# Layer norm of tokens 512 to 2047 from column tiles of x, and a written order for all five engines, in the opening of an attention and MLP kernel

## The chip, the core and the metric

The kernel runs on one core of a Trainium2 chip. Five engines work side by side, each through its own queue in order: PE (TensorE, matrix products), DVE (VectorE), ACT (ScalarE), POOL (GpSimd) and SP (SyncE, which here only issues transfers). The metric is the device time of one execution in microseconds (us); lower is better. Times of the trace count from the start of its span.

## The reference, cut to what matters

The input x has 2048 tokens of 512 features. It is normalised without weights, goes through attention of 32 heads with 16 features each and through an MLP with 1792 hidden features, and the two meet in a gate:

```python
xn = _layernorm(x, axis=-1)          # (x - mean) / sqrt(var + eps)
s = _A_ref(xn, A_wqkv, A_wo)         # softmax(q k^T / 4) v, then @ wo
g = _silu(_B_ref(xn, B_w1, B_b1, B_w2, B_b2))   # relu(xn @ w1 + b1)^2 @ w2 + b2
return x + s * g
```

Everything is float32. The kernel keeps that precision on PE by splitting each operand into a high part (rounded to PE's format) and a low part (the rest), and adds three products: high by high, high by low, low by high.

## The kernel before

**Layout.** The 2048 tokens form four chunks c of 512, and 16 tiles t of 128. For the products, the normalised x has to stand with its features on the partitions: `xTs[c]` holds, for a chunk, [128 partitions, high and low, 4 blocks of features (KO = 4), 512 tokens]. From it come q and k, by tiles ("qk", m, c) of 128 output rows (m = 0 to 3 is q, 4 to 7 is k, eight heads each), and v, by tiles ("v", c, tt) of 128 tokens. A tile is 12 matmuls of 512 columns (4 blocks by three products; L1207 for q and k, L1273 for v), and 24 of 256 columns for m = 0 and 4 of chunk 0.

**Opening, up to the first rounds.** SP loads 16 tiles of x (L1361, 256 KB each), and between them the weights `wm` (k and q of the first eight heads), `wv` (v) and later `wr` (the others). Each x tile has its tokens on the partitions and passes through this chain: statistics on DVE (`ln_stats`, L1369, L1371), square root on ACT (L1373), reciprocal and shift on DVE (L1378, L1379), normalisation on ACT (L1387; on DVE, L1383, for the first two tiles), four transposes on PE into a bank of PSUM (`ln_high`, L1394), the high part by ACT out of PSUM (L1396) and the low part by DVE (`ln_low`, L1402), which subtracts the high part from the bank. The weights are split by ACT and POOL (`split_w`, L1136, L1137, L116, L117). Between the transposes, `pump(n)` puts a few matmuls of the product tiles on PE, by a table of numbers for each tile. A done product tile is copied out of PSUM by ACT, split by POOL (`split`, L116 and L117: a copy to the high part, then a subtraction) or by ACT and DVE (`split_psum`, L122, L123), and stored to DRAM by SP (L1162, L1285).

**Order.** In this part the order of PE, ACT, DVE and POOL is as the code is written (`manual_schedule`); the queue of SP is ordered by a scheduler. SP's DMAs and, in the change, ACT's share eight semaphores in turn, so that a DMA waits until the one that had its semaphore before it has landed. By L1553 the twelve loads of k for the first four heads (`load_k`, L181, 128 KB each, 16 partitions) and those of q (`load_q_pair`, L170) are asked for; with them come the biases b1 and b2 (L1542, L1545).

**What follows.** From L1572 on come the rounds (`side_rounds`, L1303): PE is split into two row halves, on which the other product tiles go side by side with the first score tiles, whose maxima DVE takes (`max_mm`, L401, L408). The rounds need k of the first four heads in `kas` (tile ka) and q in `qms` (tile qm). Behind them the loop over 512 steps does scores, exp, the products with v, and the MLP between them. Rounds and loop are the same before and after the change.

The lines at which the opening hands a tile on:

```python
when_done(lambda: qk_done(m, c, ps, quick, 0))   # L1215: copy out, split, store
if i >= 4:
    pump({4: 6, 7: 14, 8: 12}.get(i, 8 if i < 7 else 7 if i < 11 else 6))
```

Of the kernel before, what the change touches and what calls it, by code (L numbers as in the profile page):

```python
# [9 lines left out]
F32 = mybir.dt.float32  # L10
# [63 lines left out]
def kernel(  # L74
    ctx: ExitStack,
    tc: tile.TileContext,
    x: bass.AP,
    wqkv: bass.AP,
# [18 lines left out]
    sp_d = dram.tile([S, D], F32, name="sp_d")  # L97
    xn_d = dram.tile([2, P, KO, S], F32, name="xn_d")
# [33 lines left out]
    with ExitStack() as ph:  # L132
# [42 lines left out]
        def load_k(qd, n):  # L175

            p, j, i = n // 6, n // 3 % 2, n % 3
            if n % 6 == 0:
                kas[qd, p] = ring("ka")
            h = 4 * qd + 2 * p + j  # L180
            nc.sync.dma_start(  # L181
                kas[qd, p][64 * j + DH * i : 64 * j + DH * (i + 1), :].bitcast(F32),
                k_d[h // 8][i % 2, (h % 8) * DH : (h % 8 + 1) * DH, :],
            )
# [13 lines left out]

        def load_q(u, name):
            tiles = []  # L200
            for p in range(2):
                load_q_pair(u, name, p, tiles)
            return tiles
# [928 lines left out]
        def split_w(dst, kos, cols, raw, pool=False):  # L1132
            if pool:
                split((dst[:, 0, kos, cols], dst[:, 1, kos, cols]), raw)
                return
            nc.scalar.activation(dst[:, 0, kos, cols], raw, AF.Copy)  # L1136
            nc.gpsimd.tensor_tensor(  # L1137
                dst[:, 1, kos, cols], raw, dst[:, 0, kos, cols].bitcast(F32), op=ALU.subtract
            )

        def load_w(name, width, at, kos=(KO,)):
            raw = st.tile([P, KO, width], F32, name=name)
            k0 = 0
            for n in kos:
                nc.sync.dma_start(
                    raw[:, k0 : k0 + n],
                    wqkv[:, at + k0 * width : at + (k0 + n) * width].rearrange(
                        "p (k n) -> p k n", n=width
                    ),
                )  # L1150
                k0 += n
            return raw
# [28 lines left out]
        held = []  # L1181
        hold = [True]

        def when_done(fn):
            if hold[0]:
                held.append(fn)
            else:
                fn()

        def let_go():  # L1190
            while held:
                held.pop(0)()

# [8 lines left out]
        def qk_tile(m, c):  # L1202
            ps = qkv_bank()

            for n0, n1 in ((0, 256), (256, 512)) if c == 0 and m % 4 == 0 else ((0, 512),):
                for out_, lh, rh, first_, last_ in qk_terms(m, c, ps):
                    nc.tensor.matmul(  # L1207
                        out_[:, n0:n1], lh(slice(0, P)), rh(slice(0, P))[:, n0:n1],
                        start=first_, stop=last_,
                    )  # L1210
                    if not last_ or n1 < 512:
                        yield
            quick = m % 4 == 0 and not hold[0]

            when_done(lambda: qk_done(m, c, ps, quick, 0))  # L1215
            yield

        def qk_done(m, c, ps, quick, wait):
            hl = hlp.tile([P, 2, 512], F32R, name="hl")
            if quick:  # L1220
                split_psum(hl[:, 0], hl[:, 1], ps)
            else:
                raw = hlp.tile([P, 512], F32, name="raw", bufs=2)
                nc.scalar.activation(raw, ps, AF.Copy)
                split((hl[:, 0], hl[:, 1]), raw)
            later(wait, lambda: qk_store(m, c, hl))
# [726 lines left out]
```

## Time and profile before

| | us |
|---|---|
| time, median of 3 runs (1571.22 to 1571.72) | 1571.31 |
| the profiled execution, its own time | 1571.16 |
| its span, from the first to the last instruction | 1569.3 |
| opening: up to the first round on PE (L1303) | 0 to 62.36 |
| rounds, about | 62 to 160 |
| loop and end | 160 to 1569.3 |

A row of the timeline gives start and duration in us, engine, line, operation, out<-in with shapes, and the count of merged instructions; in brackets how long the engine stood idle before, and what released it. In the table by stage each engine has its busy time and its count of instructions in the stretch, then come the granted clock of PE (1.00 is full), the share of time that the DMA engines were busy, and GB/s. In a row of the groups, busy time and mean duration in ns stand behind the bar. In a row of the waits stand the sum in us, how often, and the longest.

### The profile page before, as it was taken

To read this page: it belongs to the slowest core of one execution; us is meant where nothing else is said; L and a number is where in the kernel's file an instruction comes from. 1 tells how busy PE (TensorE), PEld (TensorE's weight loads), DVE (VectorE), ACT (ScalarE), POOL (GpSimd) and SP (SyncE) were. 2 spreads that over 40 slices of the span, in tenths; PEclk is the share of its full clock that TensorE was granted. 3 is DMA by queue.
4 is the path that set the end of the run, shared out by engine and by line. 5 is a ranking of instruction groups with operands and counts; after the bars stand their busy time and mean duration, and the time that the engine had idled before them with its cause. 6 is when DMAs were issued, how large, how long until landed. Compare 5 with 4: busy or idle time off the path is not lost.

```text
span 1569.3 us, 34206 instructions
## 1 busy us (share of the span) xinstructions
PE 1557.0 (99%) x12364; PEld 872.9 (56%) x12364; DVE 1342.3 (86%) x2307; ACT 1279.3 (82%) x2507; POOL 805.9 (51%) x824
## 2 busy tenths in 40 slices
PE   8999999999999999999999999999999999999998
PEld 7899755555555555555555555555555555555553
DVE  7377899999989998999899999998999999887765
ACT  7222788888889888888898888888888888888886
POOL 6346787348645543354465434545654345654621
PEclk9999999999999999999999999999999999999999
DMA  8967666224544531345244322533552143347665
GB/s 296 255 237 233 198 200 183 51 58 129 173 111 137 148 88 38 77 142 129 73 137 139 71 56 72 157 103 81 145 150 57 37 107 90 75 119 220 205 203 179
DMA packets 152216, 210.11 MB, mean 134 GB/s; under 512 B 58192, under 2 KB 71248, under 8 KB 150480
## 3 DMA queue, kind: packets, MB, share of 16 engines
q1 hardware_dynamic: 151904, 207.67, 46.5%
q8 instruction: 98, 1.61, 0.4%
q14 instruction: 70, 0.57, 0.1%
q10 hardware_dynamic: 144, 0.26, 0.0%
HBM read 141.56 MB, written 63.68 MB: 131 GB/s over the span
## 4 chain that ended last, share of the span: by engine, by line
PE 98%; DVE 1%; DMA 1%; issue 0%; ACT 0%; SPq 0%; DVEq 0%
PE se L487 17%; PE se L1434 12%; PE po L487 9%; PE pd_t L275 8%; PE pm_t L275 8%; PE pm_t L401 7%; PE pm_t L1434 7%; PE se L401 5%; PE pm_t L487 5%; PE pm_t L1303 4%; PE po L1434 4%; PE pd_t L401 2%; PE pm_t L243 2%; PE po L401 1%; PE pd_t L1303 1%; PE se L1273 1%
## 5 line engine op out<-in xcount | busy, mean ns | idle before, releaser
L408 DVE TENSOR_REDUCE mx<-pm_t 128x1 f32<-128x512 f32 x898 | 590.2, 682 | 50.3 <-PE pm_t L401 36.7
L1446 ACT ACTIVATE pt<-se 128x512 f32<-128x512 f32 x983 | 570.5, 623 | 30.4 <-PE pm_t L275 10.2
L408 DVE TENSOR_REDUCE mx<-se 128x1 f32<-128x512 f32 x716 | 478.3, 684 | 90.5 <-PE se L401 62.5
L1434 PE MATMUL se<-qe,ka 64*128 64x512 f32 x1086 | 434.4, 414 | 0.0
L401 PE MATMUL pm_t<-ka,qm 64*128 64x512 f32 x898 | 347.8, 398 | 0.0
L1446 ACT ACTIVATE pt<-pm_t 128x512 f32<-128x512 f32 x546 | 326.9, 622 | 8.9 <-PE pm_t L275 3.9
L1434 PEld LDWEIGHTS se<-qe,ka 64*128 64x128 f32 x1086 | 195.6, 184 | 201.6 <-ACT pt L1446 129.6
L487 PE MATMUL se<-pt,v 128*32 128x512 f32 x2224 | 282.1, 602 | 0.0
L401 PE MATMUL se<-ka,qm 64*128 64x512 f32 x716 | 281.8, 412 | 0.0
L1683 POOL TENSOR_TENSOR sum<-sum,sum 128x512 f32<-128x512 f32 x99 | 127.8, 1291 | 186.3 <-ACT sum L1682 185.9
L1683 POOL TENSOR_TENSOR ot<-ot,sum 128x512 f32<-128x512 f32 x99 | 127.7, 1290 | 180.2 <-ACT sum L1682 180.0
L1434 PE MATMUL pm_t<-qe,ka 64*128 64x512 f32 x575 | 219.0, 407 | 0.0
L275 PE MATMUL pm_t<-w2t,hT 64*128 64x512 f32 x780 | 206.6, 398 | 0.0
L1446 ACT ACTIVATE pt<-po 128x512 f32<-128x512 f32 x299 | 186.7, 625 | 7.8 <-PE pm_t L275 3.8
L401 PEld LDWEIGHTS pm_t<-ka,qm 64*128 64x128 f32 x898 | 164.0, 184 | 35.6 <-DVE mx L408 4.0
L275 PE MATMUL pm_t<-xc,w1s 64*128 64x512 f32 x672 | 177.3, 396 | 0.0
L275 PE MATMUL pd_t<-xc,w1s 64*128 64x512 f32 (+1 forms) x672 | 170.9, 388 | 0.0
L408 DVE TENSOR_REDUCE mx<-pd_t 128x1 f32<-128x512 f32 x233 | 158.7, 681 | 1.5 <-PE pd_t L401 1.5
L408 DVE TENSOR_REDUCE mx<-po 128x1 f32<-128x512 f32 x201 | 137.4, 683 | 22.2 <-PE po L401 18.7
L275 PE MATMUL pd_t<-w2t,hT 64*128 64x512 f32 x564 | 149.3, 397 | 0.0
L401 PEld LDWEIGHTS se<-ka,qm 64*128 64x128 f32 x716 | 131.4, 184 | 21.0 <-DVE mx L408 7.9
L275 PEld LDWEIGHTS pm_t<-w2t,hT 64*128 64x128 f32 x780 | 139.5, 184 | 4.4
(225 smaller groups left out, 2956.9 us busy)
## 6 DMA issues: line engine op xcount, KB each, us to landing
w1s<-w_d SPq DMA_DIRECT2D x84, 256.0 KB
w2t<-w_d SPq DMA_DIRECT2D x42, 512.0 KB
qm<-q_d SPq DMA_DIRECT2D x384, 32.0 KB
ka<-k_d SPq DMA_DIRECT2D x96, 128.0 KB
qe<-q_d SPq DMA_DIRECT2D x384, 32.0 KB
q_d<-hl SPq DMA_DIRECT2D x16, 512.0 KB
g<-g_d SPq DMA_DIRECT2D x32, 256.0 KB
k_d<-hl SPq DMA_DIRECT2D x15, 512.0 KB
```

What stands on the lines that cost most here:

```text
L243: mm = nc.tensor.matmul(out_() if callable(out_) else out_, lh(r), rh(r), start=first_ and lane == 0, stop=last_ and lane == 1, skip_group ...
L275: mm = nc.tensor.matmul(out_() if callable(out_) else out_, lh(r), rh(r), start=first_ and lane == 0, stop=last_ and lane == 1, skip_group ...
L401: nc.tensor.matmul(ps, qms[u][p][64 * j : 64 * j + 64, qb * P : (qb + 1) * P], kas[qd, p][64 * j : 64 * j + 64, kc * 512 : (kc + 1) * 512] ...
L408: return nc.vector.tensor_reduce(mxs[u][:, c, kc : kc + 1], ps, axis=AX.X, op=ALU.max)
L487: nc.tensor.matmul(po[32 * j : 32 * j + 32, :], vs[qd][:, (4 * kb + j) * VW : (4 * kb + j) * VW + 32], pts[j], start=first, stop=last, ski ...
L1273: nc.tensor.matmul(out_, lh(slice(0, P)), rh(slice(0, P)), start=first_, stop=last_)
L1303: mm = nc.tensor.matmul(out_, lh(r), rh(r), start=first_ and lane == first, stop=last_ and lane != first, skip_group_check=True,)
L1434: nc.tensor.matmul(se, kas[qd, j // 2][b : b + 64, kb * P : (kb + 1) * P], qes[u][j // 2][b : b + 64, :], start=True, stop=True,)
L1446: return nc.scalar.activation(pts[j], se, AF.Exp, scale=0.25)
L1683: nc.gpsimd.tensor_tensor(pos["sum"], pos["sum"], part, op=ALU.add)
```

## The change

Tokens 0 to 511 (tiles 0 to 3) keep the old way. Tokens 512 to 2047 come in six groups g of 256, each loaded twice: as rows (`load_rows`, tile xg, two tokens on a partition) for the statistics alone, and as columns (`load_columns`, tile xc, features on the partitions), out of a second copy of x that the host lays out that way. Mean and standard deviation are taken from the rows on DVE and ACT, written to DRAM (`row_out`, st_d) and read back spread over all partitions (`row_in`, sb, 256 KB), both from ACT's queue. DVE then subtracts and multiplies the columns in place (`column_norm`), ACT makes the high part and DVE the low part, both out of SBUF. No transposes are needed for these tokens.

The opening is now one list in which the calls of all engines stand in one order, SP's too. wv is split by ACT and POOL in place of POOL alone. All q and k tiles are split by POOL but ("qk", 4, 3), which ACT and DVE split out of PSUM. k of chunks 0 to 2 is loaded from DRAM in two steps (`load_k` with columns); that of chunk 3 goes straight from SBUF to SBUF (`move_k`), and half of the 24 transfers of the last step are issued by ACT. The copy of `xTs[0]` into ring ka and the biases are asked for behind them (`keep_first`, `load_bias`).

The new functions, and two stretches of the list:

```diff
+        def load_rows(g):
+            rows[g] = xp.tile([P, 2, D], F32, name="xg", bufs=3)
+            nc.sync.dma_start(
+                rows[g], xf[512 + g * 256 : 768 + g * 256, :].rearrange("(p j) d -> p j d", j=2)
+            )
+        def load_columns(g):
+            columns[g] = xp.tile([P, KO, 256], F32, name="xc", bufs=3)
+            nc.sync.dma_start(columns[g], xc[g])
+        def row_stats(g, j):
...
+            nc.vector.bn_stats(stats, rows[g][:, j])
+            nc.vector.bn_aggr(moments[g][:, :, j], stats)
+        def row_root(g):
+            m = moments[g][:, 1]
+            nc.scalar.activation(m, m, AF.Sqrt, bias=eps_t)
+        def row_scale(g):
+            m = moments[g][:, 1]
+            nc.vector.reciprocal(m, m)
+        def row_out(g):
+            nc.scalar.dma_start(st_d[g], moments[g])
+        def row_in(g):
+            spread[g] = xp.tile([P, P, 2, 2], F32, name="sb", bufs=3)
+            nc.scalar.dma_start(
+                spread[g].rearrange("p a s j -> p (a s j)"),
+                st_d[g].rearrange("a s j -> (a s j)")[None, :].to_broadcast([P, 512]),
+            )
+        def column_norm(g):
+            v = columns[g].rearrange("p k (a j) -> p k a j", j=2)
+            for i, op in enumerate((ALU.subtract, ALU.mult)):
+                nc.vector.tensor_tensor(
+                    v, v, spread[g][:, None, :, i, :].to_broadcast([P, KO, P, 2]), op=op
+                )
+        def column_high(g):
+            c, h = divmod(g + 2, 2)
+            nc.scalar.activation(
+                xTs[c][:, 0, :, h * 256 : (h + 1) * 256], columns[g], AF.Copy
+            )
+        def column_low(g, eng):
...
+            eng.tensor_tensor(
+                xTs[c][:, 1, :, sl], columns[g], xTs[c][:, 0, :, sl].bitcast(F32),
+                op=ALU.subtract,
+            )
+        def low_w(dst, kos, cols, raw):
             nc.gpsimd.tensor_tensor(
+                dst[:, 1, kos, cols], raw[:, kos], dst[:, 0, kos, cols].bitcast(F32),
+                op=ALU.subtract,
+            )
+        def move_k(n, eng):
+            p, j, i = n // 6, n // 3 % 2, n % 3
+            h = DH * (2 * p + j)
+            eng.dma_start(
+                kas[0, p][64 * j + DH * i : 64 * j + DH * (i + 1), 3 * 512 :].bitcast(F32),
+                outs["qk", 4, 3][0][h : h + DH, i % 2].bitcast(F32),
+            )
...
+        matmuls(("v", 0, 1), 12)
+        copy_out(("v", 0, 0))
+        low_w(wr_t, slice(0, 1), slice(0, 3 * P), raw_r)
...
+        copy_out(("qk", 4, 3), True)
+        load_k(0, 0, 2, 3, nc.sync)
+        fill_ring("qe", 2, 0.0)
+        load_k(0, 3, 2, 3, nc.scalar)
...
+        move_k(9, nc.scalar)
+        store(("qk", 4, 3))
+        copy_out(("v", 1, 3))
```

How the instructions stand on two engines at the places the steps speak of. On PE, from the tiles of chunk 0 on, the transposes (L1394) of later tokens stood between the matmuls before (xT_193, 194, 195 and 192 are chunks 0 to 3):

```order
L1207 MATMUL se<-xT_193,wa_t 128x256 x2
L1273 MATMUL se<-wa_t,xT_193 128x512 x10
L1394 MATMUL pm_t<-ident,xn 128x128 x4
L1273 MATMUL se<-wa_t,xT_193 128x512 x7
L1394 MATMUL pm_t<-ident,xn 128x128 x4
L1273 MATMUL se<-wa_t,xT_193 128x512 x7
L1394 MATMUL pm_t<-ident,xn 128x128 x4
L1207 MATMUL se<-xT_194,wa_t 128x512 x6
```

From its first transposes to the end of the opening, PE now has this (xT_199, 200, 201 and 198 are chunks 0 to 3):

```order
L1408 MATMUL pm_t<-ident,xt 128x128 x8
L1238 MATMUL se<-xT_199,wa_t 128x256 x12
L1408 MATMUL pm_t<-ident,xt 128x128 x8
L1238 MATMUL se<-xT_199,wa_t 128x256 x36
L1238 MATMUL se<-wa_t,xT_199 128x512 x48
L1238 MATMUL se<-xT_200,wa_t 128x512 x24
L1238 MATMUL se<-wa_t,xT_200 128x512 x24
L1238 MATMUL se<-xT_201,wa_t 128x512 x12
L1238 MATMUL se<-wa_t,xT_200 128x512 x12
L1238 MATMUL se<-xT_198,wa_t 128x512 x12
L1238 MATMUL pd_t<-wa_t,xT_200 128x512 x12
L1238 MATMUL po<-xT_201,wa_t 128x512 x12
```

Twelve groups of four transposes are gone, and q and k of a chunk stand behind all v tiles of chunk 0; the last k tile, of chunk 3 (xT_198), has three tiles behind it where it had seven.

On DVE, in the middle of the opening, each tile of 128 tokens had this before:

```order
L1378 RECIPROCAL rstd<-rstd 128x1
L1379 TENSOR_SCALAR rstd<-mv,rstd 128x1
L1402 TENSOR_TENSOR xT_194<-pm_t,xT_194 128x4x128
L1369 BN_STATS stats<-xt 128x6
L1371 BN_AGGR mv<-stats 128x2
```

Now, from the statistics of group 3 to those of group 4 (xg are rows, xc columns, sb the spread statistics):

```order
L1437 BN_STATS stats<-xg 128x6
L1438 BN_AGGR mvg<-stats 128x2
L1461 TENSOR_TENSOR xc<-xc,sb 128x1024 x2
L1446 RECIPROCAL mvg<-mvg 128x2
L1461 TENSOR_TENSOR xc<-xc,sb 128x1024 x2
L1474 TENSOR_TENSOR xT_200<-xc,xT_200 128x4x256 x2
L1437 BN_STATS stats<-xg 128x6
```

The low part is taken from SBUF (xc) and no longer from PSUM (pm_t), in passes of 1024 elements, and the two passes on xc are new on DVE.

On POOL, the splits at the same time are these: the end of those of the first two q and k tiles, then the low parts of wr, memsets, and the first of the splits of three more tiles. Before, wr stood behind these memsets and behind two more splits.

```order
L119 TENSOR_TENSOR hl<-raw,hl 128x512
L1145 TENSOR_TENSOR wr_t<-wv,wr_t 128x384 x4
L162 MEMSET ka_215 32x2048 x2
L162 MEMSET qm_211 32x512 x2
L162 MEMSET qm_212 32x512 x2
L118 TENSOR_SCALAR hl<-raw 128x512
L119 TENSOR_TENSOR hl<-raw,hl 128x512
```

More of the change, by code (lines that the diff above doesn't have):

```diff
@@ L97 @@
     sp_d = dram.tile([S, D], F32, name="sp_d")
+    st_d = [dram.tile([P, 2, 2], F32, name=f"st_d{g}") for g in range(6)]
     xn_d = dram.tile([2, P, KO, S], F32, name="xn_d")
@@ L1200, in qkv_bank, with qk_done @@
             return pd.tile([P, 512], F32, name="pd_t")
[L1202 to L1218, printed above, removed]
-            hl = hlp.tile([P, 2, 512], F32R, name="hl")
[L1220 to L1225, printed above, removed]
+        def qk_done(m, c, ps, wait):
+            hl = hlp.tile([P, 2, 512], F32R, name="hl")
+            raw = hlp.tile([P, 512], F32, name="raw", bufs=2)
+            nc.scalar.activation(raw, ps, AF.Copy)
+            split((hl[:, 0], hl[:, 1]), raw)
             later(wait, lambda: qk_store(m, c, hl))
@@ L1529 @@
-        let_go()
-        hold[0] = False
-        while ahead:
-            pump(1)
+        qms[0] = []
+        raw_m = w_tile("wm", 2 * P)
+        raw_v = w_tile("wv", D)
+        load_x(0)
+        load_x(1)
+        load_w(raw_m, 0, 0, 2)
+        load_w(raw_m, 0, 2, 2)
+        load_x(2)
+        load_x(3)
+        load_w(raw_v, KO * 2 * P, 0, 2)
+        ln_stats(0)
+        load_rows(0)
+        load_w(raw_v, KO * 2 * P, 2, 2)
+        ln_stats(1)
+        ln_root(0)
+        load_rows(1)
```

515 lines of the change are left out of this document (338 added, 177 removed).

## The prediction

> **What bounds the kernel now.** First the head of the page and the chain of work that ended last: which engine sets the end?
>
> ```profile
> span 1569.3 us, 34206 instructions
> ...
> PE 98%; DVE 1%; DMA 1%; issue 0%; ACT 0%; SPq 0%; DVEq 0%
> ```
>
> PE carries 98% of the chain. A busy PE isn't a PE at its peak, so next comes the table by stage, cut where the kernel's stages change.
>
> ```profile
> core 0: us, PE busy (x) PEld busy (x) DVE busy (x) ACT busy (x) POOL busy (x), PEclk, DMA share, GB/s
> 19.20:62.30 43.10, 43.10 (x206) 34.90 (x204) 16.74 (x44) 22.98 (x45) 26.06 (x30) 1.00 0.93 250
> 62.30:160.00 97.70, 97.69 (x838) 91.34 (x839) 75.36 (x120) 24.31 (x43) 46.87 (x55) 1.00 0.74 245
> ```
>
> The change touches only what comes before 62.3 us. From 62.3 to 160 PE is busy throughout at the granted clock 1.00, and DVE for 75 of 98 us, so work that starts earlier there ends earlier. The question is thus one number: when does PE start its first interleaved round (L1303, 62.36 us)? From 19.2 on PE never waits while DVE is busy for 16.74 of 43.1 us. The timeline of PE shows what fills it:
>
> ```profile
> 19.21 2.48 PE L1273 MATMUL se<-wa_t,xT 128*128 128x512 f32 x10
> 21.52 0.60 PE L1394 MATMUL pm_t<-ident,xn 128*128 128x128 f32 x4
> ...
> 36.65 0.60 PE L1394 MATMUL pm_t<-ident,xn 128*128 128x128 f32 x4
> ...
> 45.47 8.56 PE L1273 MATMUL se<-wa_t,xT 128*128 128x512 f32 x36
> 53.87 2.96 PE L1273 MATMUL pd_t<-wa_t,xT 128*128 128x512 f32 x12
> ...
> 62.36 0.50 PE L1303 MATMUL pm_t<-wa_t,xT 64*128 64x512 f32 x1
> ```
>
> 36 matmuls take 53.87 - 45.47 = 8.40 us, so a tile of 12 takes 2.80. From 19.21 to 62.36 there are 14 tiles (39.2 us) and nine groups of four transposes (21.52 the first, 36.65 the last): (43.15 - 39.2) / 9 = 0.44 us for a group.
>
> **Removed from PE.** Twelve groups of transposes go: 12 x 0.44 = 5.3 us, three of them before 19.21 (where v(0, 0) could then start at about 17.9) and nine behind. PE by itself would reach its rounds at 17.9 + 39.2 = 57.1 us. With them go ACT's twelve normalisations and twelve copies out of PSUM; ACT isn't late here (22.98 of 43.1 us).
>
> **Added to DVE.** DVE now does for each 256 tokens two subtract/multiply passes and one low-part pass of 1024 elements. Before, a tile of 128 tokens cost it this:
>
> ```profile
> 29.40 0.68 DVE L1369 BATCH_NORM_STATS2 stats<-xt 128x6 f32<-128x512 f32 x1
> 30.12 0.18 DVE L1371 BATCH_NORM_AGGREGATE mv<-stats 128x2 f32<-128x6 f32 x1
> 30.22 0.13 DVE L1378 RECIPROCAL rstd<-rstd 128x1 f32<-128x1 f32 x1
> ```
>
> Statistics take 30.22 - 29.40 = 0.82 from start to start, and a reciprocal 0.13. A DVE pass with both inputs in SBUF stands only at the kernel's end, and the same rows show what POOL does to it:
>
> ```profile
> 1514.72 0.65 DVE L958 TENSOR_TENSOR g<-g,s 128x512 f32<-128x512 f32 x1
> 1515.29 0.15 DVE L1796 TENSOR_SCALAR seen<-se 128x1 f32<-128x1 f32 x1
> ...
> 1516.56 0.69 DVE L955 TENSOR_TENSOR g<-se,g 128x512 f32<-128x512 f32 x1
> 1517.28 1.07 DVE L958 TENSOR_TENSOR g<-g,s 128x512 f32<-128x512 f32 x1
> ...
> 1535.22 1.82 DVE L958 TENSOR_TENSOR g<-g,s 128x512 f32<-128x512 f32 x2
> ```
>
> ```profile
> 1517.07 0.73 POOL L117 TENSOR_TENSOR hl<-ot,hl 128x256 fp32r<-128x256 f32 x1
> ...
> 1535.30 1.20 POOL L117 TENSOR_TENSOR hl<-tot,hl 128x256 fp32r<-128x256 f32 x1
> ```
>
> From start to start 512 elements take 1515.29 - 1514.72 = 0.57 us, so I take 1.14 for 1024 (an upper value, since a fixed part is doubled), and 0.11 more where the next pass needs this one's result (1517.28 - 1516.56 = 0.72 for an instruction of 0.69). A pair is 1.25 + 1.14 = 2.39. DVE has, from the first pair on, six pairs (14.3), six low parts (6.8), the statistics of the last two groups (4 x 0.82 = 3.3) and three reciprocals (0.4): 24.8 us in a row, since the list puts them back to back.
>
> **Where that row starts.** It stands behind the statistics of group 3, whose rows the queue of SP asks for behind 5.77 MB: four tiles of x (1.05), wm and wv (1.57), and rows and columns of three groups (3.15).
>
> ```profile
> 0.00:5.00 5.00, 0.00 (x0) 0.00 (x0) 2.07 (x14) 1.58 (x2) 4.27 (x8) 1.00 0.66 193
> 5.00:10.00 5.00, 2.96 (x12) 2.44 (x13) 3.83 (x12) 2.71 (x6) 1.44 (x3) 1.00 1.00 365
> 10.00:15.00 5.00, 4.96 (x34) 4.75 (x33) 4.50 (x16) 4.07 (x8) 4.83 (x6) 1.00 1.04 392
> ```
>
> By 15 us 5 x (193 + 365 + 392) = 4.75 MB had come. At 392 GB/s rows 3 (0.52 MB more, 6.29 in all) land at 18.9, or at 19.6 if one spread tile sb of 0.26 MB comes between. Two statistics later (1.64) the row starts at 20.5 to 21.2; I take 20.9. Alone it would end at 20.9 + 24.8 = 45.7.
>
> **The new wait.** DVE's new passes meet POOL's splits. In the rows above a DVE pass that started 0.21 us into a POOL pass lost 0.38 us (1.07 against 0.69) of the remaining 0.52; two passes at 1535.22 took 1.82, where 0.57 + 0.69 = 1.26 was due, and lost 0.56 to a POOL pass that lasts 0.73 undisturbed. POOL lost too (1.20 against 0.73). So the two take turns, and DVE loses 0.73 to 0.77 of POOL's time. This is told also by the Trainium skill, SBUF — State Buffer, section "Who interferes with whom": a DVE instruction with two SBUF inputs and a GpSimd instruction that reads SBUF exclude each other, and the second is blocked until the first is done; the trace agrees but for the quarter of the time that stays hidden. By the page the whole of POOL's time would be lost, and the sum below would be 2.4 us higher. POOL has, in the time of DVE's row, by its order, four low parts of wr and the splits of three tiles of q and k:
>
> ```profile
> L117 POOL TENSOR_TENSOR hl<-raw,hl 128x512 fp32r<-128x512 f32 x4 | 5.2, 1292 | 0.3
> ...
> L1137 POOL TENSOR_TENSOR wr_t<-wv,wr_t 128x384 fp32r<-128x384 f32 x4 | 3.9, 1011 | 3.5 <-ACT wr_t L1136 3.5
> L116 POOL TENSOR_SCALAR hl<-raw 128x512 fp32r<-128x512 f32 x4 | 2.5, 620 | 7.6 <-ACT raw L1224 7.5
> ```
>
> That is 4 x 1.01 + 3 x (0.62 + 1.29) = 9.8 us. The first four follow ACT's copies of wr (loaded behind rows 3, so about 22 to 27 us) and lie on the first two pairs and low parts; each split follows its tile on PE by a copy, when DVE is at the pairs or low parts of the next groups. With 0.75: 7.4 us; the ends are nothing and 9.8. The row ends at 45.7 + 7.4 = 53.1. POOL's memsets read no tile; I leave them out, an assumption.
>
> **Who waits for the row's end.** The second matmul of qk(4, 3) needs the last low part. Behind it PE has 11 matmuls and three tiles: 11 x 0.233 + 8.4 = 11.0. That gives 64.1. On the way PE waits at qk(4, 1), qk(4, 2) and qk(4, 3), each time for a low part.
>
> **The moves of k.** ACT gets twelve DMAs of 32 KB between its copies of qk(4, 3) and v(1, 3); the last tile on PE, v(2, 0), needs v(1, 3) out of its bank. Rows of before for such DMAs into 16 partitions (the time SP took, and the stage's GB/s):
>
> ```profile
> 50.81 6.46 SPq L181 DMA_DIRECT2D ka<-k_d  x12
> ```
>
> ```profile
> 55.00:60.00 5.00, 5.00 (x23) 4.01 (x22) 0.00 (x0) 0.89 (x2) 2.12 (x2) 1.00 1.06 131
> ```
>
> At 131 GB/s all 24 (0.79 MB) take 6.0 us; the last can be asked for when 16 have landed, after 4.0. With ACT's copies at both ends (0.7 + 0.6) that is 5.3 us, less than the two tiles (5.6) that cover it: nothing. At SP's 6.46 us for twelve it is 7.8: 2.2 us late. I take 0.7. Should the cover go, each microsecond more is one for PE. The bias loads, too, change places:
>
> ```profile
> 20.75 1.18 SPq L1542 DMA_DIRECT2D b_t<-in_B_b_dram  x1
> 21.98 5.26 SPq L1545 DMA_DIRECT2D b_t<-in_B_b_dram  x1
> ```
>
> They held SP for 6.4 us while PE had transposes to do, and now hold it at the rounds' start. Behind them wait the stores of v(1, 3), of q(0, 2) and of the v tiles, and the second load of wr. The covers are the seven buffers of the v tiles (a tile each 2.8 us, so some 17 us) and the first three maxima, which come before ACT asks for wr. Priced at nothing; if wr came later than that, ACT's copies of the next banks would stand behind it, a microsecond for each one late. The stores and spills of chunks 0 and 1 only come later, and their readers are in the rounds.
>
> **Sum.** 64.1 + 0.7 = 64.8 against 62.36: +2.4 us. The profiled execution took 1571.16 us (its span of 1569.3 and 1.9 around it), 0.15 below the median of 1571.31. Forecast: 1571.16 + 2.4 = 1573.6 us, no change that can be measured well: the transposes' gain goes into DVE's wait for POOL. Its own range comes from the lock (5.0 to 9.8 us) and the moves (0 to 2.2): 1571 to 1577.
>
> **Rivals.** *DVE keeps up* (chance 0.37): POOL's work falls beside statistics, or DVE's passes on 1024 elements are shorter than twice 0.57. For it: DVE has no two-input pass in 3.3 us of statistics, and the order leaves some room there; before, DVE was busy for only 39% of this stage. Against it: the disturbed rows above, and 24.8 us with no gap. Without any loss the row ends at 45.7, and PE's own time decides: 57.1 + 0.7 = 57.8, 4.6 us earlier, 1566.6 us. Half the loss would be about 1570.
>
> *The statistics come late* (0.13, slower): rstd and mean go out to DRAM and come back spread over all partitions, both on ACT's queue, where each read waits for the write.
>
> ```profile
> SPq L478 <- DMA sh_d<-sh: 36.9, 28, 4.5
> ```
>
> The like round trip made SP wait 1.3 us in the mean (36.9 / 28) and 4.5 at most. Group 0's statistics are ready at about 13.9 us (the last copies of x tiles 2 and 3); with issues of 0.35 and 0.53 and two landings of 4.5, sb would come at 23.8 in place of 20.9, and everything behind it 2.8 us later: 1576.5. It decides from about 3.1 us a landing on; at 1.3 nothing is late.
>
> **Chances.** Forecast 0.50, DVE keeps up 0.37, statistics late 0.13. About 0.2% (3.1 us) is what a measurement of this kernel can tell from no change, so faster is below 1568.2 and slower above 1574.4. Faster: most of the first rival, 0.32. Slower: three tenths of the forecast and nearly all of the second, 0.26. Same: 0.42. The range leaves out the ends of the rivals: 1566.3 to 1576.8; the likeliest alone 1571 to 1577.
>
> **What would show it.** Twelve groups of transposes gone and PE's tiles at 2.80 us: step one. Gaps on PE of 2 to 3 us ahead of qk(4, 1), qk(4, 2) and qk(4, 3), released by DVE's low part: the row decides; no gaps, the first rival. DVE passes on xc of about 1.2 us alone, and 2.0 or more where a POOL pass lies beside them: the turns. DVE idle ahead of its first pair until a DMA of sb: the second rival. A gap ahead of v(2, 0), released by ACT: the moves. The forecast is wrong if the first round starts before 60 us, or if the rounds behind it take other than their 97.7 us.

## The result, and the profile after

The changed kernel takes 1598.28 us (median of four runs, 1596.98 to 1598.47) against 1571.26 us of the kernel before on the same chip: ratio 1.017, 95% interval 1.0153 to 1.0188. It is 27 us slower. The forecast was 1573.6 us, no change, with a range up to 1576.8: wrong by 25 us and outside its range.

The head of the page, its chain of work, and the two stages of the prediction, now of the changed kernel:

```profile
span 1596.6 us, 34128 instructions
...
PE 94%; DMA 3%; DVE 1%; issue 0%; ACT 0%; SPq 0%; ACTq 0%; POOL 0%; DVEq 0%; POOLq 0%
```

```profile
19.20:62.30 43.10, 31.67 (x109) 23.57 (x108) 24.62 (x30) 13.69 (x24) 21.33 (x19) 0.84 0.78 239
62.30:160.00 97.70, 88.20 (x669) 80.92 (x670) 62.70 (x97) 18.94 (x32) 42.27 (x52) 0.95 0.71 227
```

PE was busy for all 43.1 us of the first stage before; now for 31.67, at a granted clock of 0.84 in place of 1.00. DVE, the engine that the prediction feared, is busy for only 24.62. DMA has 3% of the chain. The timeline of PE says where (L1238 is the opening's product tiles, L1314 the first round):

```profile
18.06 2.96 PE L1238 MATMUL se<-wa_t,xT 128*128 128x512 f32 x12
...
27.44 8.62 PE L1238 MATMUL se<-wa_t,xT 128*128 128x512 f32 x24 [2.94 <-ACT raw L1264]
37.24 0.51 PE L1238 MATMUL se<-xT,wa_t 128*128 128x512 f32 x1 [1.18 <-ACT xT L1467]
...
55.39 0.80 PE L1238 MATMUL se<-xT,wa_t 128*128 128x512 f32 x1 [5.68 <-ACT xT L1467]
56.65 4.72 PE L1238 MATMUL se<-xT,wa_t 128*128 128x512 f32 x11 [0.46 <-DVE xT L1474]
...
69.74 0.80 PE L1238 MATMUL se<-xT,wa_t 128*128 128x512 f32 x1 [5.58 <-ACT xT L1467]
71.00 4.41 PE L1238 MATMUL se<-xT,wa_t 128*128 128x512 f32 x11 [0.46 <-DVE xT L1474]
...
84.44 4.61 PE L1238 MATMUL pd_t<-wa_t,xT 128*128 128x512 f32 x12 [3.45 <-ACT vt L1254]
88.97 0.50 PE L1314 MATMUL pm_t<-wa_t,xT 64*128 64x512 f32 x1
```

The first round starts at 88.97 us, before at 62.36: 26.6 us later. What follows it is unchanged: from the first round to the end of the span before took 1569.3 - 62.36 = 1506.9 us and the changed kernel 1507.6. So the whole loss is in the opening. PE's waits in that stretch, summed by what ended them, are these:

```profile
PE se L1238 <- ACT xT L1467: 12.4, 3, 5.7
PE pd_t L1238 <- ACT vt L1254: 3.5, 1, 3.5
PE se L1238 <- ACT raw L1264: 3.4, 2, 2.9
PE se L1238 <- DVE xT L1474: 1.7, 3, 0.8
```

That is 21.0 us of idling behind v(0, 0), whose start at 18.06 is the predicted one (17.9). The 14 tiles from there are 39.2 us of work, so of the 70.9 us up to the first round 70.9 - 39.2 - 21.0 = 10.7 are left. About 9.6 of them are slow tiles behind the four long gaps: the two tiles behind the first take 8.62 us in place of 5.6, the others 4.4 to 5.1 from start to start in place of 2.80. The granted clock of PE (third number from the end) tells them apart, first behind the gap at 27.44, then for tiles that follow others:

```profile
27.44:33.00 5.56, 5.56 (x13) 4.40 (x14) 1.89 (x3) 3.87 (x8) 5.44 (x6) 0.50 0.99 253
43.95:49.50 5.55, 5.55 (x25) 4.32 (x23) 3.87 (x4) 0.54 (x1) 2.74 (x2) 1.00 1.05 363
```

Three of the four lines name ACT. What ACT itself waits for is in its timeline (ACTq rows are DMAs that it issues: L1449 stores the statistics to st_d, L1453 reads them back into sb):

```profile
14.62 0.35 ACTq L1449 DMA_DIRECT2D st_d<-mvg  x1
...
19.88 0.35 ACTq L1453 DMA_DIRECT2D sb<-st_d  x1
...
20.78 0.60 ACT L1264 ACTIVATE raw<-se 128x512 f32<-128x512 f32 x1 [3.86 <-DMA st_d<-mvg]
...
26.79 0.60 ACT L1264 ACTIVATE raw<-se 128x512 f32<-128x512 f32 x1 [5.23 <-DMA st_d<-mvg]
...
41.74 0.33 ACTq L1449 DMA_DIRECT2D st_d<-mvg  x1
...
48.08 0.34 ACTq L1453 DMA_DIRECT2D sb<-st_d  x1
...
48.96 1.06 ACT L1467 ACTIVATE xT<-xc 128x1024 fp32r<-128x1024 f32 x1 [6.17 <-DMA st_d<-mvg]
```

The read-back stands in ACT's queue until the store has landed: 5.3 us for group 0 (14.62 to 19.88) and 6.3 for group 4 (41.74 to 48.08). Behind the read-backs stand copies that free banks of PE (20.78; that of 26.79, behind group 1, ends PE's gap of 2.94 us) and high parts that DVE's low parts and PE need (48.96; the next, at 54.28, ends PE's gap of 5.68 us). DVE's row of passes was no row either:

```profile
25.81 2.49 DVE L1461 TENSOR_TENSOR xc<-xc,sb 128x1024 f32<-128x1024 f32 x2 [2.45 <-DMA st_d<-mvg]
...
32.13 3.96 DVE L1461 TENSOR_TENSOR xc<-xc,sb 128x1024 f32<-128x1024 f32 x2 [3.56 <-DMA sb<-st_d]
...
55.37 1.22 DVE L1474 TENSOR_TENSOR xT<-xc,xT 128x1024 fp32r<-128x1024 f32 x1 [4.10 <-ACT xT L1467]
...
66.11 2.49 DVE L1461 TENSOR_TENSOR xc<-xc,sb 128x1024 f32<-128x1024 f32 x2 [7.12 <-DMA xc<-in_A_x_columns_dram]
68.52 2.43 DVE L1474 TENSOR_TENSOR xT<-xc,xT 128x1024 fp32r<-128x1024 f32 x2
```

It begins at 25.81, waits again for the read-back (32.13), for ACT's late high parts (55.37) and for columns 5 (66.11), and ends at 70.95, where the prediction had 53.1.

### The profile page after: what moved, and what is told of

Read it like the earlier page. It is cut to its first block, busy times and chain, and to the rows that moved or that the text cites. A ratio compares the mean times of both kernels' runs of the same rounds, so it can differ in the third digit from the quotient of the medians.

```text
span 1596.6 us, 34128 instructions
## 1 busy us (share of the span) xinstructions
PE 1562.4 (98%) x12316; PEld 873.5 (55%) x12316; DVE 1354.6 (85%) x2293; ACT 1271.1 (80%) x2487; POOL 811.3 (51%) x824
## 4 chain that ended last, share of the span: by engine, by line
PE 94%; DMA 3%; DVE 1%; issue 0%; ACT 0%; SPq 0%; ACTq 0%; POOL 0%; DVEq 0%; POOLq 0%
PE se L484 17%; PE se L1493 12%; PE po L484 9%; PE pm_t L272 8%; PE pd_t L272 7%; PE pm_t L398 7%; PE pm_t L1493 6%; PE se L398 5%; PE pm_t L484 5%; PE pm_t L1314 4%; PE po L1493 4%; PE pd_t L398 2%; PE pm_t L240 2%; DMA st_d<-mvg 1%; PE pd_t L1314 1%; PE po L398 1%
```

## The experiments

The theory after this reading: the trip of the statistics through DRAM is the cause, by its length and by ACT's standing behind it. The rivals: the lock between DVE and POOL (the prediction's own reason), the load of columns 5, the moves of k on ACT, and PE's clock. Each run is judged by its ratio and by the start of the first round in its profile. In all of them, but for one run named below and the last, 1507 to 1508 us follow that start, so a microsecond there is one of time. The intervals of the first four ratios are wide, because one run of the kernel before took 1589.27 us where the six others took 1570.6 to 1571.8. It lowers those ratios too: from the medians they would be 1.0125, 1.0141, 1.0146 and 1.0155.

How far two profiles of the same opening differ can be read from the last run, which changes nothing in it: its first round came at 87.57 us, 1.4 earlier than in the changed kernel, and its gap ahead of qk(4, 2) was 2.68 us in place of 5.68. Gains of 2 us below are not far above that.

| run | first round, us | ratio (95%) |
|---|---|---|
| before | 62.36 | 1 |
| changed | 88.97 | 1.017 (1.0153 to 1.0188) |
| read-back waits for no store | 80.81 | 1.0106 (1.005 to 1.0161) |
| read-back on POOL's queue | 84.87 | 1.0122 (1.0067 to 1.0177) |
| moves of k all on SP | 82.93 | 1.0128 (1.0062 to 1.0194) |
| low parts of wr left out | 86.53 | 1.0137 (1.0081 to 1.0192) |
| columns 5 ahead of qm | 86.71 | 1.0152 (1.0138 to 1.0166) |
| statistics spread by PE | 69.54 | 1.0047 (1.0034 to 1.0061) |
| the same, with three repairs | 67.73 | 1.0039 (1.0026 to 1.0051) |
| 60 more matmuls in the gaps | 86.93 | 1.016 (1.0144 to 1.0175) |
| spread, three repairs, ACT's copies first | 60.45 | 1.0015 (1.0006 to 1.0024) |
| spread by PE, copied to SBUF | 72.56 | 1.0069 (1.0053 to 1.0084) |
| the repairs without the spread | 83.55 | 1.0151 (1.0137 to 1.0164) |
| copies first, biases later | 62.22 | 0.9996 (0.9987 to 1.0005) |

**The read-back waits for no store.**

```diff
-                st_d[g].rearrange("a s j -> (a s j)")[None, :].to_broadcast([P, 512]),
+                xf[g : g + 1, :].to_broadcast([P, 512]),
```

> The read-back of the statistics takes its 512 numbers from a row of x in place of st_d, so ACT's queue never stands before a store that has not landed; the store itself stays, and so do all bytes. This leaves out the right statistics. If the wait for the stores (25 us of idle on ACT in the first 90 us of the changed kernel) opens PE's gaps, those at 27.4, 37.2 and 55.4 us go (2.9 + 1.9 + 6.2 = 11 us), and part of the one at 69.7 (6.0 us), since SP's queue waits on the same landings: first round at 72 to 79 us instead of 89, time 10 to 17 us under the changed kernel's, ratio to the kernel before 1.006 to 1.011. If DVE and POOL holding each other is what counts, 0 to 2 us: ratio 1.015 to 1.018. If the moves of k on ACT are, no change either.

The run leaves out the right statistics. The first round came 8.2 us earlier, less than the expected 10 to 17 and far more than the 0 to 2 of the rivals. Two of PE's gaps in this run:

```profile
32.07 0.50 PE L1238 MATMUL se<-xT,wa_t 128*128 128x512 f32 x1 [1.89 <-ACT xT L1467]
...
61.75 0.80 PE L1238 MATMUL se<-xT,wa_t 128*128 128x512 f32 x1 [8.53 <-ACT xT L1467]
```

The gaps for the bank (27.4 us) and for qk(4, 2) (55.4 us) are gone, so ACT's standing behind the stores made those. But the one for qk(4, 3) grew from 5.6 to 8.5: everything ahead of it is earlier and columns 5 are not early enough. What is left of the trip is the read-back itself, 7.4 us from its issue (16.38) to the first subtraction (23.83).

**The read-back on POOL's queue.**

```diff
-            nc.scalar.dma_start(
+            nc.gpsimd.dma_start(
                 spread[g].rearrange("p a s j -> p (a s j)"),
```

> The read-back is issued by POOL's queue in place of ACT's; the numbers are right, the trip is as long as before, but ACT's copies of PSUM are no longer queued behind it. If it is ACT's standing in order that costs (copies of PSUM and high parts late), the gap at 27.4 us goes, those at 37.2 and 55.4 shrink to what DVE is late: 6 to 12 us under the changed kernel, ratio 1.009 to 1.014. If it is the length of the trip itself (DVE gets its numbers late), 0 to 3 us: ratio 1.015 to 1.018. If POOL's splits, now behind the same waits, hold SP's stores and with them columns 5, slower than the changed kernel: above 1.018.

4.1 us earlier, between two of the expectations. The gap for the bank is gone, but one of 7.51 us stands ahead of qk(4, 1): group 0's store still took 5.6 us (14.56 to 20.20) and the read-back 8.2 (to 28.43). Another queue frees ACT; the trip stays as long.

**The moves of k on SP**, all twelve that ACT issued.

```diff
-        load_k(0, 3, 2, 3, nc.scalar)
+        load_k(0, 3, 2, 3, nc.sync)
...
-        move_k(3, nc.scalar)
+        move_k(3, nc.sync)
```

> The 12 loads and moves of k that the change issues on ACT go back to SP. If ACT's 8.2 us of issues (75.5 to 83.7) hold the copy of v(1,3) for which PE idles 3.45 us, the gap at 84.4 goes: 3 to 4 us under the changed kernel, ratio 1.015. If SP is then late with k for the first maxima, the first round starts no earlier, or its maxima wait: 0 or slower, ratio 1.017 or above. The prediction priced these moves at 0.7 us.

6.0 us earlier, and 4.1 by the medians, where 3 to 4 were expected. The gap of 3.45 us is gone, and the last tile takes 2.95 in place of 4.61, since no gap has lowered the clock; from the start of v(1, 3) to the first round it is 8.4 us against 13.7. With the slow tile that they cause, the moves cost 5.3 us of the 26.6, not 0.7.

**The low parts of wr left out.** The run sets this part of the weights to zero.

```diff
+        nc.gpsimd.memset(wr_t[:, 1, :, : 3 * P].bitcast(F32), 0.0)
...
-        low_w(wr_t, slice(0, 1), slice(0, 3 * P), raw_r)
```

> The four low parts of wr on POOL are left out (that part of the weights is zero), so nothing of POOL stands beside normalisation 1. If the lock between DVE and POOL were worth the 7.4 us of the prediction: 3 us or more under the changed kernel, ratio 1.015 or less. If it is the stores' landing, normalisation 1 takes 2.5 in place of 3.96 us and the time moves by 0 to 1.5 us: ratio 1.016 to 1.018.

Normalisation 1 took 2.49 us in place of 3.96, and the first round came 2.4 us earlier, with the gaps of the trip still there (3.03 us for the bank, 6.54 ahead of qk(4, 2)). That is between the two expectations (0 to 1.5, 3 or more) and near the difference of two profiles. The lock is there, and its part beside wr is at most a tenth of the loss; the splits of q and k still disturb normalisation 3 (3.68 us). The run with the copy in SBUF below measures the whole.

**Columns 5 ahead of qm.**

```diff
-        load_q_pair(0, "qm", 0, qms[0])
...
-        load_q_pair(0, "qm", 1, qms[0])
...
         load_columns(5)
+        load_q_pair(0, "qm", 0, qms[0])
+        load_q_pair(0, "qm", 1, qms[0])
```

> SP's queue loads the columns of normalisation 5 ahead of the twelve loads of qm in place of behind them; nothing else changes. If PE's gap at 69.7 us (6.0 us, and a slow clock behind it) is the place of that load in SP's queue, the load goes out near 51 instead of 61 us, the gap closes: 4 to 7 us under the changed kernel, ratio 1.011 to 1.014. If the statistics alone are late, the columns wait for the same thing: 0 to 1 us, ratio 1.016 to 1.017. If k then comes late for the first maxima, slower than that.

The load went out at 50.1 and the gap for qk(4, 3) fell from 5.6 us to 0.3, as expected. But the time fell by less than the expected 4 us:

```profile
81.29 5.49 PE L1238 MATMUL pd_t<-wa_t,xT 128*128 128x512 f32 x12 [8.18 <-ACT vt L1254]
```

PE is now at v(1, 3) at 67.38 us in place of 75.25, but SP asks for the last loads of k at 73.96, as in the changed kernel (73.95): the loads of qm and the first twelve of k still stand ahead of them. ACT's own transfers of k begin at 73.97 and end at 80.59 in place of 83.74, and the copy of v(1, 3) behind them ends a gap of 8.18 us. One late transfer hid the next one.

**The statistics spread by PE.** Four transposes of a repeated column put the four rows of statistics on all partitions in a PSUM bank; st_d and sb are gone.

```diff
+            spread[g] = pm.tile([P, 512], F32, name="pm_t").rearrange("p (s j a) -> p s j a", s=2, j=2)
+            for s in range(2):
+                for j in range(2):
+                    nc.tensor.transpose(
+                        spread[g][:, s, j], moments[g][:, s, j : j + 1].to_broadcast([P, P]), ident
+                    )
```

> The statistics no longer go through DRAM: TensorE transposes each column of four numbers' worth, repeated 128 times, into a PSUM bank, four transposes a normalisation (24 x 0.11 = 2.6 us of PE), and DVE reads them there. The numbers are right. If the trip is the cause of the gaps at 27.4, 37.2 and 55.4 us, all three go and nothing else does: 9 to 13 us of gaps and slow clock less the 2.6 us, 7 to 11 us under the changed kernel, ratio 1.010 to 1.013; normalisations at 2.5 us even beside POOL, since one of DVE's operands is then PSUM. If only DVE's row counts, 0 to 3 us.

19.4 us earlier, twice what was expected. From v(0, 0) on, PE has two long gaps left, for columns 5 (3.54 us) and behind the moves of k (2.17 us). The expectation had counted only PE's gaps that lead straight to the store. But in the changed kernel SP waits on the trip too, since its transfers share semaphores with ACT's; among its own largest waits in the first 100 us there are these:

```profile
SPq L172 <- DMA sb<-st_d: 6.7, 2, 3.8
SPq L1517 <- DMA sb<-st_d: 6.6, 2, 5.5
...
SPq L1277 <- DMA st_d<-mvg: 5.1, 1, 5.1
```

L172 are the loads of qm ahead of columns 5, so SP passes the lateness on to columns 5 and k. In this run those waits are gone, and SP asks for columns 5 at 44.11 us in place of 61.13. The run takes away more than the wait, though: the 1.6 MB of the six read-backs don't move, and DVE's normalisations, with one operand in PSUM, no longer wait for POOL (measured below).

**The same, with three repairs**: columns 5 ahead of qm as above, and these two.

```diff
+        row_root(3)
+        row_scale(3)
         column_norm(0)
-        row_root(3)
...
-        row_scale(3)
...
         move_k(5, nc.scalar)
+        copy_out(("v", 1, 3))
...
         store(("qk", 4, 3))
-        copy_out(("v", 1, 3))
```

> The spread by TensorE, the columns of 5 ahead of qm, the copy of v(1,3) ahead of ACT's second half of the moves of k, and the statistics of group 3 ahead of normalisation 0. If these three causes (trip, columns 5, moves) with the slow clock behind each gap are the whole loss, first round at 57.1 (PE alone, by the prediction) + 2.6 + 1 to 5 of gaps = 61 to 65 us, against 62.4 of the kernel before: ratio 0.999 to 1.002. If something else is behind it (DVE's row beside POOL), first round at 68 or later: 1.004 and above.

Ratio 1.0039 and first round at 67.73, just short of the bounds (1.004, 68) for "something else". PE has one gap left in the opening, 4.31 us ahead of v(2, 0), behind ACT's moves of k. The DVE row isn't it: DVE was done at 50.5 us.

**60 more matmuls in the gaps.**

```diff
+                nc.tensor.matmul(pt, wa_t[:, 0, 0, :P], xTs[0][:, 0, 0], start=True, stop=True)
...
+        warm_up(20)
         matmuls(("qk", 4, 2), 12)
```

> The changed kernel with 60 matmuls of 512 columns more (8, 20, 20 and 12, some 14 us of PE at full clock, results unused) put ahead of the tiles for which PE idles: v(0,2), qk(4,2), qk(4,3) and v(2,0). The waits stay what they are. If the low granted clock (0.70 to 0.85) and the tiles of 4.4 us behind the gaps come from PE's having idled, work in the gaps keeps it up: tiles of 2.8 us behind them, 4 to 7 us under the changed kernel though it computes more, ratio 1.012 to 1.015. If the clock has another cause, no gain, or up to 5 us slower where the extra work outlasts a gap: ratio 1.017 to 1.020.

```profile
50.88 4.81 PE L1407 MATMUL pm_t<-xT,wa_t 128*128 128x512 f32 x20
55.53 2.94 PE L1238 MATMUL se<-xT,wa_t 128*128 128x512 f32 x12
...
69.37 0.79 PE L1238 MATMUL se<-xT,wa_t 128*128 128x512 f32 x1 [3.48 <-ACT xT L1472]
70.63 5.06 PE L1238 MATMUL se<-xT,wa_t 128*128 128x512 f32 x11 [0.47 <-DVE xT L1479]
```

Where the extra work (L1407) fills a gap, the tile behind it takes 2.94 us at a granted clock of 1.00; where 3.48 us of gap remain, 11 matmuls take 5.06, at 0.50 up to 75.00. So idling is what lowers the clock. This agrees with the Trainium skill, TensorE: Matmul & The Clock Gate, Part 1, which halves the clock after an idle window of about 3.4 us and restores it after as long a busy one. The length of one gap doesn't decide here: 2.94 us was already enough in the changed kernel (24 matmuls in 8.62 us at 27.44) and 2.25 in the run with the moves on SP (11 matmuls in 5.06 at 55.43), while 2.91 in the run with columns 5 first was not (24 in 5.85 at 27.84). The gain was only 2.0 us and the ratio can't be told from the changed kernel's, against an expected 4 to 7: a quicker tile that has to wait for columns 5 anyway gains nothing. PE starts qk(4, 3) 0.4 us earlier, and the last tile, 2.94 us in place of 4.61, gives the rest.

**The spread, the three repairs, and ACT's copies first**, with the store of qk(4, 2) right behind its split. Against the run with three repairs:

```diff
         copy_out(("qk", 4, 3), True)
+        copy_out(("v", 1, 3))
...
         move_k(5, nc.scalar)
-        copy_out(("v", 1, 3))
+        copy_out(("qk", 0, 2))
...
-        copy_out(("qk", 0, 2))
```

> As the run with the spread by TensorE and the other repairs, but ACT copies v(1,3) out before all of its moves of k and qk(0,2) in their middle, and the store of k(2) goes out right behind its split. If the last gap (4.3 us, with a tile of 4.6 behind it, at 63.2 us) is ACT's moves standing ahead of a copy, it goes: first round at 61 to 64 us against 67.7, 4 to 6 us less, ratio 0.999 to 1.002. If k itself is late, the gap moves behind the first round's first maximum: 0 to 2 us less, ratio 1.003 to 1.004.

No gap at all from v(0, 0) to the first round, which starts at 60.45, earlier than before. Yet 1513 us follow, 6 more than elsewhere. (This profiled execution, 1575.34 us, was the slowest of the run's eleven; their median is 2.1 us less.) PE, ACT and SP in the rounds:

```profile
86.24 2.93 PE L1313 MATMUL pm_t<-wa_t,xT 64*128 64x512 f32 x12 [2.70 <-ACT raw L1187]
```

```profile
83.94 1.76 ACT L1141 ACTIVATE wr_t<-wv 128x384 fp32r<-128x384 f32 x4 [8.12 <-DMA wv<-in_A_wqkv_dram]
```

```profile
71.39 3.88 SPq L1529 DMA_DIRECT2D b_t<-in_B_b_dram  x1
...
76.27 0.49 SPq L1133 DMA_DIRECT2D wv<-in_A_wqkv_dram  x1
```

The second load of wr stands behind the biases on SP, and ACT idles 8.1 us until it has landed.

**Copies first, biases later.** Against the run before:

```diff
-        load_bias()
...
+            if g == 5:
+                load_bias()
```

> As the run before with ACT's copies first, but the two loads of biases, which stand on SP's queue from 70.4 to 75.3 us ahead of the second load of wr (issued at 76.3, landed at 83.9, and PE idles 2.7 us at 86.2 with a slow clock behind), are issued some rounds later. If those issues are what makes wr late, the gap and its slow clock go: first round at 60.5 as before, and from there the 1507 us that all other kernels of this study take to the end: a span of 1567 to 1568, ratio 0.998 to 0.9995. If wr is late by the moves of k on SP instead, ratio 1.000 to 1.001.

The gap in the rounds is gone, and 1507 us follow the first round again. In the profiled execution that round started at 62.22, not 60.5, with a gap of 1.74 us ahead of the second matmul of qk(4, 3): columns 5 came 0.8 us later than in the run before (44.89 against 44.13), and DVE's two low parts behind them took 3.77 us in place of 2.5, beside a split of POOL. Ratio 0.9996: no difference from the kernel before that can be measured, and the best version found.

**Spread by PE, copied to SBUF.** ACT copies each spread into SBUF, so that the normalisation has two operands of SBUF, as in the changed kernel.

```diff
+            nc.scalar.activation(
+                spread[g].rearrange("p a s j -> p s j a"), pt, AF.Copy
+            )
```

> As the spread by TensorE alone, but ACT copies each spread from PSUM into SBUF (six copies), so that the subtraction and the multiplication of the normalisations read two operands of SBUF again, as in the changed kernel. The trip stays away: only DVE's and POOL's standing in each other's way comes back. If that is worth the 7.4 us of the prediction on the way to the first round, ratio 1.009 to 1.010 (the spread alone: 1.0047). If it costs only where the two meet (1.3 to 1.5 us each, two to four times, partly hidden), 0 to 3 us: ratio 1.005 to 1.007.

DVE's groups of normalisations and low parts, first with the operand in PSUM, then with the copy in SBUF:

```profile
L1459 DVE TENSOR_TENSOR xc<-xc,pm_t 128x1024 f32<-128x1024 f32 x12 | 14.5, 1213 | 6.9 <-DMA xc<-in_A_x_columns_dram 6.7
L1472 DVE TENSOR_TENSOR xT<-xc,xT 128x1024 fp32r<-128x1024 f32 x6 | 7.3, 1238 | 0.5 <-ACT xT L1465 0.5
```

```profile
L1463 DVE TENSOR_TENSOR xc<-xc,sb 128x1024 f32<-128x1024 f32 x12 | 18.1, 1511 | 3.6 <-DMA xc<-in_A_x_columns_dram 3.4
L1476 DVE TENSOR_TENSOR xT<-xc,xT 128x1024 fp32r<-128x1024 f32 x6 | 10.0, 1686 | 0.3 <-ACT xT L1469 0.3
```

The lock costs DVE 12 x (1.511 - 1.213) + 6 x (1.686 - 1.238) = 6.3 us, near the predicted 7.4, and POOL too: its four low parts of wr go from 1.02 to 2.00 us each. The low parts read two operands from SBUF in both runs, so their 2.7 us come only from where POOL's work lay. The first round moves by 3.0 us (ACT's six copies in it), the ratio by 0.0022.

**The repairs without the spread.** The edits of the run with three repairs, without those of the spread:

```diff
+        row_root(3)
+        row_scale(3)
         column_norm(0)
-        row_root(3)
...
-        row_scale(3)
...
-        load_q_pair(0, "qm", 0, qms[0])
...
-        load_q_pair(0, "qm", 1, qms[0])
...
         load_columns(5)
+        load_q_pair(0, "qm", 0, qms[0])
+        load_q_pair(0, "qm", 1, qms[0])
...
         move_k(5, nc.scalar)
+        copy_out(("v", 1, 3))
...
         store(("qk", 4, 3))
-        copy_out(("v", 1, 3))
```

> The changed kernel with the other three repairs (columns of 5 ahead of qm, the copy of v(1,3) ahead of half of ACT's moves, statistics of group 3 ahead of normalisation 0) and the trip through DRAM as it is. If the trip is the main cause, these repairs alone are worth little, because what they free is late by the trip anyway: 3 to 7 us under the changed kernel, ratio 1.012 to 1.015, 13 us or more above the run that has the spread as well (1.0039). If the causes were independent, 9 us or more: 1.011 or less.

1.0151: the three repairs are worth 3 us while the trip is there, and the same three are worth 1.0047 - 1.0039, 1.3 us, without it. The other way round, taking the trip away is worth 1.017 - 1.0047, 19.3 us, without the repairs and 1.0151 - 1.0039, 17.6 us, with them. So the trip is the main cause either way, and the two add up nearly; that the trip hides what these three repairs free is not shown. In their last form, with ACT's copies first and the biases later, the repairs are worth 1.0047 - 0.9996, 8 us, without the trip: here one late transfer after another had to go, as in the run with columns 5 first.

**The same trip in a quiet place.** In the changed kernel, far behind the opening, SP's queue stores 128 x 16 bytes and reads them back to all partitions three times.

```diff
+                nc.sync.dma_start(t, b2_t[:, :4].rearrange("p (s j) -> p s j", j=2))
+                nc.sync.dma_start(
+                    b2_t, t.rearrange("a s j -> (a s j)")[None, :].to_broadcast([P, 512])
+                )
```

> The changed kernel, and far behind the opening, where DMA is quiet, the same trip three times more on SP's queue: 128 x 16 bytes stored, 128 x 2 KB read back from them, each waiting for the one before (b2 serves as the tile and is loaded again). If the store's 5.2 to 6.3 us in the opening come of the traffic, it lands here in 1.5 to 2.5 us, and the read-back in 2 to 3 instead of 5.7. If they come of the store's own shape (128 pieces of 16 bytes), it takes 5 us or more here too. The time says nothing: SP's queue stands still for the trips.

The issues on SP's queue, each waiting for the one before, and then the DMA share (last but one) from the issue of each of the three stores to the issue that waits for it:

```profile
1432.75 0.73 SPq L1963 DMA_DIRECT2D t_d<-b_t  x1
1439.03 0.32 SPq L1964 DMA_DIRECT2D b_t<-t_d  x1
1442.31 0.32 SPq L1963 DMA_DIRECT2D t_d<-b_t  x1
1444.20 0.32 SPq L1964 DMA_DIRECT2D b_t<-t_d  x1
1447.71 0.32 SPq L1963 DMA_DIRECT2D t_d<-b_t  x1
1449.11 0.32 SPq L1964 DMA_DIRECT2D b_t<-t_d  x1
1453.21 0.32 SPq L1967 DMA_DIRECT2D t_d<-b_t  x1
```

```profile
1432.75:1439.03 6.28, 6.28 (x54) 3.64 (x52) 4.83 (x10) 5.30 (x12) 1.88 (x2) 1.00 0.72 247
1442.31:1444.20 1.89, 1.89 (x20) 1.14 (x14) 1.08 (x2) 1.62 (x4) 0.98 (x1) 1.00 0.04 1
1447.71:1449.11 1.40, 1.40 (x16) 0.51 (x12) 1.40 (x3) 1.40 (x5) 0.00 (x0) 1.00 0.06 2
```

The place happened to hold both cases. The first store met 247 GB/s of other transfers and took 6.3 us to land; the second and third, with next to nothing beside them, took 1.9 and 1.4. The read-backs took 3.3, 3.5 and 4.1 us there, more than the 2 to 3 expected, against 5.7 to 8.2 in the opening. It is the traffic, not the shape of the store. The first store stood behind other loads of its own queue (SP's), while the stores of the opening are on ACT's: whether a store waits for its queue or for the DMA engines is not shown.

## Why the prediction was wrong, step by step

**Removed from PE: right.** v(0, 0) starts at 18.06 (17.9 predicted), tiles that nothing disturbs follow each other by 2.8 us.

**DVE's passes: right.** 1.21 us each in the mean with no lock; a pair 2.43 to 2.49 (2.39 predicted), a low part 1.22 (1.14).

**"24.8 us in a row", from 20.9: the step that failed.** The sum held the loads and DVE's own work and put nothing for the waits of the trip. The row starts at 25.81, 4.9 us late: DVE first waits 3.35 us for ACT's square root of group 2, which stands behind the read-back of group 0 (it runs at 21.27), and then 2.45 for the spread statistics. It has 17.0 us of gaps inside: 3.6 for the read-back, 6.3 for ACT's high parts behind the stores, 7.1 for columns 5. The lock in it, at 2.9 us (12 passes of 1.455 in place of 1.213), is 4.5 less than predicted, because DVE mostly stood idle when POOL worked. 4.9 + 17.0 - 4.5 = 17.4 of the 17.9 us between 53.1 and 70.95.

**The rival "The statistics come late": the right mechanism at a small part of its price.** It had a chance of 0.13 and was to cost 2.8 us. It failed in three places. Its landing of 1.3 us came from a wait in the loop; the landings in the opening were 5.3 to 6.3 for the store and 5.7 or more for the read-back, above even its worst case of 4.5, and the quiet place shows that it is the traffic. It charged group 0 alone, as if the others were hidden behind DVE's row; behind the stores of groups 0, 1, 4 and 5 ACT idles 3.8 to 6.2 us each. And it charged DVE alone: it did not name what is queued behind the waiting read-back on ACT, copies that free PE's banks and the high parts. Taking the trip away gave back 19.4 of the 26.6 us, and 16.4 with DVE's operands both in SBUF as before (72.56).

**Behind the row, 11.0 us predicted, 18.0 measured.** Two terms were mis-sized. The moves of k at 0.7 (0 to 2.2) left a gap of 3.45: ACT's issues lasted from 75.51 to 83.74, 8.2 us, longer than the slow end of 7.8, where two tiles cover 5.6. And no term existed for PE's clock behind a gap, which made the last tiles some 3.4 us longer. In the trace of before the granted clock was 1.00 from 19.2 us to the end of the rounds, and PE had no gaps there to lower it.

**The lock: right in kind**, and on DVE nearly in size once the trip is gone: 6.3 us against 7.4. Nearly half of it fell on the low parts. On the way to the first round it is worth about 3.0 us, less than half of the 7.4 that the forecast put there.

**The biases, priced at nothing:** nothing in the changed kernel, where 1507.6 us follow the first round as before; 6 us between the two profiled executions as soon as the rest was repaired, of which 3 show in the ratios (1.0015 to 0.9996). The cover was the loss itself.

What stays open: how the 16.4 to 19.4 us of the trip divide between ACT's standing, the read-back's length, its bytes and the semaphores that SP shares with ACT. The run without the store's wait gave 8.2 of them; the rest was not taken apart. Why the repaired kernel, with 24 transposes in place of 48, is yet not faster than before can be added up from its profile, though no run tests it: of the 5.3 us saved, 2.1 go into its own spreads, 1.5 into a later start of PE's first products (10.45 us in place of 8.98) and 1.7 into the gap at qk(4, 3), which leaves nothing; its first round is 0.14 us earlier.

## What to carry to other kernels

A wait for a transfer is priced from a row in the same traffic: the store of a trip through DRAM that took 1.4 to 1.9 us in a quiet stretch took 5 to 6 where the loads of the opening filled DMA. A transfer that waits for another one does not belong in the queue of an engine that frees buffers, and a wait that comes once for each group is charged for each group, with all that is queued behind it. A few numbers on each partition can be spread over all partitions by TensorE for a third of a microsecond of its time, where the detour through DRAM took eleven.

## What the runs showed of the hardware

- The landing of a 2 KB store in 128 pieces of 16 bytes, with the DMA share over that time: 1.9 and 1.4 us at 0.04 and 0.06, 6.3 us at 0.72, and 5.3 to 6.3 us at 0.61 to 1.04 for four stores of the opening. The Trainium skill, DMA: Bandwidth & Descriptors, section "Latency and other measured facts", has access to memory at 0.2 us in the mean and 2 us under high load; the direction agrees, and the measured difference of more than 4 us is larger than that.
- DVE's passes of 1024 elements with one operand in PSUM take 1.21 us in the mean, also beside POOL's reads (two pairs in 2.44 and 2.46 us from 21.73 on, POOL's four low parts of wr from 22.64 on in 1.02 each). With both operands in SBUF the passes take 1.51 in the mean, and POOL's low parts of wr 2.00. This is as the Trainium skill has it, SBUF — State Buffer, section "Who interferes with whom".
- A transpose takes a column repeated by a step of zero as its input; four of them cost PE 0.36 us between its matmuls (16.30 to 16.66 in the last version).
